# Seven products for all four runs of W_in in the last two groups, and six in-place sums of the second matrix by adding DMAs

## The chip, the cores and the metric

The kernel runs on one core of a Trainium2 chip, in one launch. The metric is the device time of that launch in microseconds (us). Five engines work side by side, each through its own instructions in their order: TensorE (PE in the profile, its weight loads PEld), VectorE (DVE), ScalarE (ACT), GpSimd (POOL) and SyncE (SP). POOL and SP are used here almost only to issue DMAs.

## The reference, cut to what matters

```python
# q, k, v: (4, 8, 768, 64); w_in: (512, 2048); w_out: (2048, 512)
scores = q @ k.T / 8 + bias          # bias by head and distance
scores = where(is_global | is_local, scores, -1e9)   # 8 global keys, 96 local ones
x = softmax(scores) @ v              # heads side by side: (3072, 512)
h = x @ w_in
g = h - tanh(h)
out = g @ w_out                      # (3072, 512), float32
```

## The kernel before

The 3072 rows are 24 tiles of 128 (`u` = 0 to 23). A tile's scores are made against its own 128 keys (block 0) and, where it has one, the tile before it (block 1). `S` are the score matmuls, `E` the exponentials on ACT, `M` the multiplication with a mask on DVE, `AV` the product with v, `R` a reciprocal of the row sums on DVE, `N` the normalisation that writes a tile of x, `Xe` its transposition into `xT` (by PE and a copy up to tile 7, by a DMA from SP after that).

The first matrix product, x @ W_in, takes the tiles in ten groups: two of one tile, five of two tiles and, for tiles 12 to 23, groups 7, 8 and 9 of four tiles (512 rows). The 2048 columns of W_in are 16 slices of 128 (`f`); four slices are a run (`j` = 0 to 3). The direct way for a group of four is `m1`: per slice four matmuls 128x512 into one of the 8 PSUM banks, then tanh on ACT (`th`) and the subtraction h - tanh(h) on DVE (`g`), which writes the bf16 tensor `gall`. The other way takes a run at once as a product of 2 by 2 blocks by seven products instead of eight (`in_product`, `d1` to `d7`, four matmuls 128x256 each). It needs four sums of blocks of W_in per run (`v1` to `v4`, DVE), four of blocks of xT per group (`y1` to `y4`, DVE), three copies out of PSUM per group and run on ACT (`e0` to `e2`) and three additions on DVE (`q11`, `q21`, `q22`: `d_add`). A run so done holds three banks, one of which (`r`) goes to and fro between PE and ACT: product, copy, product, copy, product, copy, product. `DUNITS` lists the pairs (group, run) done in this way: runs 2 and 3 of groups 8 and 9.

The second product, g @ W_out, takes every pair of tiles (a, a + 1) as 2 by 2 blocks, again with seven products (`product`, `p1` to `p7`, eight matmuls 128x256 each), three copies (`a0` to `a2`, `keep`) and four results (`c11` to `c22`), then the stores (`st`) of two tiles of `ot`. Its operands are the blocks of `gall` and four sums of them by DVE (`n1` to `n4`, `g_sum`, 128x1024 bf16): with a11, a12 the first tile's two halves and a21, a22 the second's, n1 = a21 + a22 and n2 = n1 - a11 go to buffers `ss`, n3 = a11 - a21 is written over a21 and n4 = a12 - n2 over a12. `p7` reads n3's result, `p3` that of n4. Sums of blocks of W_out are made once (`w1` to `w4`, `w_sum`).

No scheduler sets the order. The string `ORDER` lists every step by its name, and each engine runs its own steps in the order of that list; a letter behind a slash gives the engine where there is a choice (`a` ACT, `d` DVE, `p` POOL, `s` SP). A second table, `HOMES`, gives each step's buffers and banks.

Of the kernel before, what the change touches and what calls it, by code (L numbers as in the profile page):

```python
# [27 lines left out]
Xe.5/d th.0.12 g.2.14 m1.3.6 E.6.1 g.0.12 m1.3.8 n3.0 th.3.6 lk.10 E.6.0 n2.0 m1.3.4 g.3.6 K.6/a m1.3.2 n1.2 w1.0
m1.3.12 th.3.2 lk.8 g.0.8 th.3.8 p1.0 w1.1 m1.3.10 w3.0 a0.0/a th.3.12 g.3.2 m1.3.0 lv.6 th.3.10 w2.0 p2.0 w2.1 lq.10
w3.1 p6.0 T.7 lv.7 w4.1 p7.0 g.3.8 a1.0/a V.5/a n2.2 p5.0 th.3.0 T.9 n3.2 g.3.12 p1.2 a2.0/a w4.0 p2.2 a0.2/a g.3.10  # L30
th.3.4 p6.2 c11.0 T.8 c22.0 M.6.0 p4.0 a1.2/a n4.2 p5.2 g.3.0 g.3.4 p7.2 a2.2/a c21.0 c11.2 p3.2 st.1.0/p T.10 v1.3
M.6.1 lk.12 S.7 c12.2/a c22.2 lk.14 AV.6 n4.0 E.7.1 p4.2 V.6/d lk.11 R.6 E.7.0 N.6/d m1.3.14 lk.13 M.7.1 X.6 M.7.0
th.3.14 p3.0 lq.12 Xe.6/a c21.2 g.3.14 AV.7 lq.11 c12.0/a K.7/d R.7 S.8 N.7/d lv.8 n1.4 X.7 lv.9 E.8.1 p1.4 Xe.7/d n2.4
lv.10 m1.4.8 E.8.0 v1.2 v2.3 lq.13 m1.4.10 a0.4/a M.8.1 th.4.8 K.9/a p6.4 g.4.8 th.4.10 E.9.0 g.4.10 m1.4.14 a1.4/d S.9
V.7/d th.4.14 M.9.0 T.11 g.4.14 p5.4 E.9.1 M.8.0 T.12 m1.4.4 E.10.0 n3.4 p2.4 M.9.1 st.3.0/s th.4.4 M.10.0 E.10.1 AV.8
n4.4 m1.4.0 T.13 lq.15 K.10/a R.8 a2.4/a N.8/d AV.9 th.4.0 g.4.4 p3.4 Xe.8 R.9 N.9/d m1.4.2 c12.4/a c11.4 Xe.9 m1.4.6
g.4.0 st.4.0/p th.4.2 M.10.1 lq.14 m1.4.12 th.4.6 g.4.2 lv.11 p7.4 g.4.6 th.4.12 lk.15 S.10 c22.4 V.9/d lv.13 g.4.12
p4.4 E.11.0 n1.6 st.2.0/p p2.6 E.12.0 K.11/d lv.12 n3.6 AV.10 n2.6 K.12/a E.11.1 lk.16 p1.6 R.10 c21.4 lq.16 N.10/a
m1.5.10 a0.6/d M.11.1 p6.6 c11.6 th.5.10 S.11 T.15 a1.6/d g.5.10 p5.6 E.13.1 M.12.0 T.14 m1.5.8 V.10/d n4.6 E.13.0
M.11.0 m1.5.14 Xe.10 E.12.1 M.13.1 AV.11 th.5.14 p7.6 R.11 th.5.8 a2.6/d M.12.1 N.11/a m1.5.12 V.11/d v3.2 p3.6 g.5.14  # L40
th.5.12 M.13.0 Xe.11 m1.5.0 c12.6/a c22.6 st.6.0/p g.5.8 m1.5.2 th.5.0 lv.14 T.16 g.5.12 AV.12 g.5.0 th.5.2 lq.19 m1.5.6
R.12 N.12/d lk.18 m1.5.4 th.5.6 g.5.2 lq.18 p4.6 g.5.6 th.5.4 lq.17 g.5.4 S.12 V.12/d lv.16 c21.6 p1.8 n1.8 E.14.1 lv.15
m1.6.4 a0.8/d E.14.0 K.15/d v2.2 lk.17 AV.13 n2.8 th.6.4 m1.6.14 K.14/d lk.19 R.13 E.15.0 g.6.4 p6.8 N.13/d th.6.14 T.18
p2.8 g.6.14 a1.8/a M.14.0 Xe.12 S.13 n4.8 p5.8 c11.8 E.16.1 st.5.0/s v4.3 M.14.1 m1.6.10 E.16.0 M.15.0 T.17 AV.14 n3.8
E.15.1 m1.6.12 R.14 N.14/d T.19 th.6.10 m1.6.0 M.15.1 m1.6.2 a2.8/d th.6.0 Xe.14 M.16.0 V.14/a m1.6.6 g.6.0 th.6.2 Xe.13
g.6.10 AV.15 th.6.6 m1.6.8 g.6.2 g.6.6 p3.8 th.6.8 R.15 N.15/d th.6.12 p7.8 c12.8/a g.6.8 Xe.15 K.16/a st.8.0/p p1.10
g.6.12 lv.19 c22.8 S.14 n1.10 a0.10/a lq.21 n2.10 p4.8 E.17.1 lv.17 M.16.1 p6.10 E.17.0 V.15/d lk.20 p2.10 a1.10/d lk.23
v4.2 c21.8 p5.10 K.17/d lk.21 n4.10 st.9.0/s AV.16 M.17.1 a2.10/a lv.18 E.18.0 m1.7.15 R.16 N.16/d lq.22 p3.10 th.7.15
c11.10 lq.20 g.7.15 S.15 V.16/d c12.10/d lk.22 m1.7.6 M.17.0 E.19.0 lq.23 m1.7.7 E.19.1 M.19.0 lv.20 m1.7.5 M.18.0
# [73 lines left out]
def kernel(  # L123
# [517 lines left out]
    def keep(e, a, k):  # L641
        copy(e, buf(("sn", a, k)), bank(("r", a))[:, 0:DH2])
# [187 lines left out]
```

## Time and profile before

| | |
|---|---|
| median of 3 runs | 202.43 us (202.15 to 202.67) |
| the profiled execution, time and span | 202.65 us and 200.9 us |
| granted TensorE clock | 1.0 |
| busy: PE, DVE, ACT, POOL | 194.4, 178.5, 132.6, 72.9 us |
| bytes moved by DMA | 27.36 MB |

The span is what the trace shows of the kernel from its first to its last event; 1.75 us of the profiled execution's time lie around it. Busy time is the time in which at least one of an engine's instructions ran. Since an instruction's successor on DVE or PE can begin before it ends, the distance from start to start, where an engine works without a gap, says better than the duration how much time an instruction takes up.

### The profile page before, as it was taken

The page shows a single profiled execution, that of the slowest core. Times are in us where ns is not written, and L with a number is a line of the kernel's source. Part 1 is how long each engine was busy: PE and PEld are TensorE (multiplying, and loading weights), DVE is VectorE, ACT ScalarE, POOL GpSimd, SP SyncE. Part 2 cuts the span into 40 slices and gives each one's busy share as a digit, 9 for nine tenths or more (in the row PEclk, how much of TensorE's full clock was granted, in tenths as well). Part 3 has the DMA queues.
Part 4 walks back from the last instruction along what each step waited for, and adds up shares of the span by engine and source line. Part 5 has one row for each costly group of instructions (what it writes and reads, how often), then busy time and mean ns, then how long its engine had stood idle before and what let it go on. Part 6 is the DMA issues. An engine that isn't in the chain of part 4 may idle for free.

```text
span 200.9 us, 5510 instructions
## 1 busy us (share of the span) xinstructions
PE 194.4 (97%) x2195; PEld 155.5 (77%) x2195; DVE 178.5 (89%) x375; ACT 132.6 (66%) x245; POOL 72.9 (36%) x93
## 2 busy tenths in 40 slices
PE   8998999999999999999999999999999999999993
PEld 2567888888878988988898655687877688778882
DVE  6685598999999998999999999999999999999841
ACT  3796889844578678958674785589678774823220
POOL 8995575350693195097009910005100002000011
PEclk9999999999999999999999999999999999999999
DMA  5999999999999999999999999932924112002223
GB/s 145 217 184 184 195 166 207 198 156 145 144 194 161 192 160 182 131 169 152 207 155 145 167 156 167 210 28 58 74 51 110 66 43 104 0 3 106 90 96 131
DMA packets 103755, 27.36 MB, mean 136 GB/s; under 512 B 93921, under 2 KB 101345, under 8 KB 103729
## 3 DMA queue, kind: packets, MB, share of 16 engines
q0 software_dynamic: 73680, 15.54, 85.9%
q1 hardware_dynamic: 29504, 10.95, 30.8%
q10 hardware_dynamic: 544, 0.52, 1.0%
q8 instruction: 17, 0.28, 0.5%
q14 instruction: 10, 0.07, 0.1%
HBM read 27.26 MB, written 6.29 MB: 167 GB/s over the span
## 4 chain that ended last, share of the span: by engine, by line
PE 69%; DMA 13%; DVE 8%; POOL 7%; issue 1%; ACT 0%; POOLq 0%; DVEq 0%
PE ps L636 31%; PE ps L470 24%; DMA w_out_bf<-in_moe_w_out_dram 7%; DMA w_in_bf<-in_moe_w_in_dram 6%; PE ps L529 6%; PE ps L420 4%; PE ps L394 4%; DVE gall L581 2%; POOL w_in_bf L343 2%; POOL vb L340 2%; POOL mem L337 1%; DVE mem L405 1%; DVE wc L608 1%; DVE ot L650 1%; DVE gall L621 1%
## 5 line engine op out<-in xcount | busy, mean ns | idle before, releaser
L470 PE MATMUL ps<-xT,w_in_bf 128*128 128x256 bf16 (+2 forms) x576 | 77.2, 284 | 1.0 <-DMA w_in_bf<-in_moe_w_in_dram 0.9
L470 PEld LDWEIGHTS <-w_in_bf 128*128 128x128 bf16 x576 | 50.2, 98 | 15.9 <-DMA w_in_bf<-in_moe_w_in_dram 1.1
L567 ACT ACTIVATE th<-ps 128x512 f32<-128x512 f32 (+1 forms) x82 | 47.1, 594 | 16.8 <-PE ps L470 14.6
L581 DVE TENSOR_TENSOR gall<-ps,th 128x512 bf16<-128x512 f32 (+1 forms) x82 | 52.9, 667 | 5.9 <-ACT th L567 5.2
L636 PEld LDWEIGHTS <-gall 128*128 128x128 bf16 x488 | 46.3, 98 | 7.6 <-issue 0.5
L401 ACT ACTIVATE mem<-ps 128x1024 bf16<-128x1024 f32 x44 | 43.3, 1027 | 7.9 <-PE ps L394 7.0
L653 POOL DMA_DIRECT2D out_dram<-ot x10 | 5.7, 572 | 105.2 <-DVE ot L650 66.9
L636 PE MATMUL ps<-w_out_bf,gall 128*128 128x256 bf16 (+1 forms) x296 | 36.4, 270 | 0.4 <-ACT ot L272 0.4
L405 DVE TENSOR_TENSOR mem<-mem,mk 128x1024 bf16<-128x1024 bf16 x40 | 26.3, 680 | 0.0
L636 PE MATMUL ps<-f,ss 128*128 128x256 bf16 x192 | 24.9, 273 | 0.0
L636 PE MATMUL ps<-wc,gall 128*128 128x256 bf16 x192 | 24.9, 273 | 0.0
L272 ACT COPY sn<-ps 128x256 f32<-128x256 f32 x23 | 8.6, 372 | 20.8 <-PE ps L636 20.8
L340 POOL DMA_DIRECT2D vb<-in_v_dram x24 | 21.5, 907 | 1.8 <-ACT sn L272 1.6
L340 POOL DMA_DIRECT2D mem<-in_q_dram x20 | 18.0, 908 | 9.5 <-PE ps L420 5.4
L636 PEld LDWEIGHTS <-ss 128*128 128x128 bf16 x192 | 18.4, 98 | 3.2
L340 POOL DMA_DIRECT2D mem<-in_k_dram x20 | 18.1, 915 | 4.6 <-DMA w_out_bf<-in_moe_w_out_dram 3.7
L650 DVE TENSOR_TENSOR ot<-ps,sn 128x256 f32<-128x256 f32 x36 | 14.6, 416 | 4.1 <-PE ps L636 3.1
L420 PEld LDWEIGHTS <-mem 128*128 128x128 bf16 x352 | 13.4, 97 | 2.3 <-ACT mem L401 0.5
L437 DVE TENSOR_TENSOR x<-ps,rden 128x512 bf16<-128x512 f32 x21 | 14.4, 687 | 0.6
L420 PE MATMUL ps<-vb,mem 128*128 128x65 bf16 x352 | 14.7, 193 | 0.1
L394 PE MATMUL ps<-mem 64*128 64x128 bf16 x352 | 13.2, 217 | 0.3 <-DVE gall L581 0.3
L394 PEld LDWEIGHTS <-mem 64*128 64x128 bf16 x352 | 10.0, 94 | 3.4 <-issue 2.4
(76 smaller groups left out, 195.6 us busy)
## 6 DMA issues: line engine op xcount, KB each, us to landing
out_dram<-ot SPq DMA_DIRECT2D x14, 256.0 KB, 2.5
vb<-in_v_dram POOLq DMA_DIRECT2D x24, 128.0 KB, 5.4
mem<-in_q_dram POOLq DMA_DIRECT2D x22, 128.0 KB, 5.8
mem<-in_k_dram POOLq DMA_DIRECT2D x22, 128.0 KB, 5.5
out_dram<-ot POOLq DMA_DIRECT2D x9, 256.0 KB, 2.6
w_out_bf<-in_moe_w_out_dram POOLq DMA_DIRECT2D x4, 512.0 KB, 10.7
w_in_bf<-in_moe_w_in_dram POOLq DMA_DIRECT2D x4, 256.0 KB, 8.2
w_in_bf<-in_moe_w_in_dram POOLq DMA_DIRECT2D x2, 512.0 KB, 11.5
```

Source lines behind the costliest of these rows:

```text
L340: eng(e).dma_start(out=dst, in_=rows_of(src, u).rearrange("h p d -> p h d"))
L394: nc.tensor.matmul(bank(("s", u, o), hh)[:, p * P : (p + 1) * P], buf(("qk", back[u] if o else u))[r, 1, p, :], buf(("qk", u))[r, 0, p, :] ...
L401: nc.scalar.activation(d, banks(("s", u, o), 0, 1), AF.Exp, bias=0.0, scale=scale)
L405: nc.vector.tensor_tensor(out=t, in0=t, in1=mk[:, mask_of(u, o)], op=ALU.mult)
L420: nc.tensor.matmul(t[:, h // (H // 2), h % (H // 2), :], buf(("p", u, o))[:, slot(h), :], buf(("v", back[u] if o else u))[:, h, 0 : Dh + 1 ...
L437: nc.vector.tensor_tensor(out=buf(("x", u)).rearrange("q (a h) d -> q a h d", a=2), in0=t[:, :, :, 0:Dh], in1=rden.to_broadcast([P, 2, H / ...
L470: nc.tensor.matmul(t[:, (f - f0) * n : (f - f0 + 1) * n], w_in_bf[j][:, c, fo : fo + P], x[:, c, 0:n], start=(c == 0), stop=(c == CD - 1),)
L529: nc.tensor.matmul(t[:, r * 2 * P : (r + 1) * 2 * P], w(r)[:, c], x[:, c], start=first and r + c == 0, stop=c == 1, skip_group_check=not f ...
L567: nc.scalar.activation(h_view(buf(("th", g, f0)), g, m), h_view(bank(("h", g, f0)), g, m), AF.Tanh, bias=0.0, scale=1.0)
L581: nc.vector.tensor_tensor(out=o, in0=v(h), in1=v(th), op=ALU.subtract)
L636: nc.tensor.matmul(bank((holder, a))[:, c0:c1], s(f), t(f)[:, c0:c1], start=first and f == 0, stop=f == HF - 1, skip_group_check=not first,)
L650: nc.vector.tensor_tensor(out=o, in0=bank((holder, a))[:, 0:DH2], in1=buf(("sn", a, k)), op=ALU.add)
```

## The change

- `DUNITS` takes all four runs of groups 8 and 9, eight units instead of four. No direct block (`m1`) of these groups is left. `v1` to `v4` are made for runs 0 and 1 too.
- The first tile of each pair (even `u`) is carried negated. Up to tile 7 the copy behind the transposition negates it (`minus`); from tile 8 on, the normalisation does (`a_N`, two SCALAR_TENSOR_TENSOR of half a tile instead of one TENSOR_TENSOR). h - tanh(h) is odd, so the first tile's blocks in `gall` are negated as well, and n2, n3 and n4 become plain additions. The signs are put right in the sums of W_out (`w2` becomes a SCALAR_TENSOR_TENSOR), in `keep` and in `result`.
- n3 and n4 of the pairs 14, 16 and 18, six sums, are DMAs from POOL that add their source to their destination in SBUF (`accum_op`); the other n3 and n4 stay on DVE.
- `ORDER` and `HOMES` are written anew, with other sides for some copies: of the 13 copies `sn` on DVE 4 are left there (one of them negating), of its 11 copies of `vb` 5; the rest goes to ACT.

```diff
 ORDER = """
...
-c12.20/a st.20.0/s p3.22.0 c21.22 c12.22.0/a p3.22.1 st.23.0/s st.22.256/p c12.22.1/d st.22.384/s
...
+p3.22.0 c12.20/a p4.22 st.20.0/s c12.22.0/a st.22.256/s p3.22.1 c21.22 c12.22.1/d st.23.0/s st.22.384/s
...
-    DUNITS = [(8, 2), (8, 3), (9, 2), (9, 3)]
+    DUNITS = [(8, 0), (8, 1), (8, 2), (8, 3), (9, 0), (9, 1), (9, 2), (9, 3)]
...
+    def minus(e, out, in_):
+        if e is ACT:
+            nc.scalar.activation(out, in_, AF.Copy, bias=0.0, scale=-1.0)
+        else:
+            eng(e).tensor_scalar(out=out, in0=in_, scalar1=-1.0, scalar2=None, op0=ALU.mult)
...
+        if u % 2 == 0 and u >= PE_X:
+            for a in range(2):
+                nc.vector.scalar_tensor_tensor(
+                    out=buf(("x", u))[:, a * H // 2 : (a + 1) * H // 2, :], in0=t[:, a, :, 0:Dh], scalar=-1.0,
+                    in1=rden[:, a].to_broadcast([P, H // 2, Dh]), op0=ALU.mult, op1=ALU.mult,
+                )
+            return
...
-        a, b = {1: (b12, b11), 2: (b22, w_half(1, x)), 3: (b22, b12), 4: (b21, w_half(2, x))}[k]
-        nc.vector.tensor_tensor(out=w_half(k, x), in0=a, in1=b, op=ALU.subtract)
+        if k == 2:
+            nc.vector.scalar_tensor_tensor(
+                out=w_half(2, x), in0=w_half(1, x), scalar=-1.0, in1=b22, op0=ALU.mult, op1=ALU.subtract)
+            return
+        a, b, o = {1: (b11, b12, ALU.subtract), 3: (b12, b22, ALU.subtract), 4: (b21, w_half(2, x), ALU.add)}[k]
+        nc.vector.tensor_tensor(out=w_half(k, x), in0=a, in1=b, op=o)
...
-            2: (lambda: buf(("ss", a, 2)), lambda: buf(("ss", a, 1)), lambda: a11, ALU.subtract),
-            3: (lambda: a21, lambda: a11, lambda: a21, ALU.subtract),
-            4: (lambda: a12, lambda: a12, lambda: buf(("ss", a, 2)), ALU.subtract),
+            2: (lambda: buf(("ss", a, 2)), lambda: buf(("ss", a, 1)), lambda: a11),
+            3: (lambda: a21, lambda: a21, lambda: a11),
+            4: (lambda: a12, lambda: a12, lambda: buf(("ss", a, 2))),
...
-        nc.vector.tensor_tensor(out=o(), in0=x(), in1=y(), op=op)
+        if e is POOL:
+            nc.gpsimd.dma_start(out=o(), in_=y(), accum_op=ALU.add)
+            return
+        nc.vector.tensor_tensor(out=o(), in0=x(), in1=y(), op=ALU.add)
...
-        nc.vector.tensor_tensor(out=o, in0=bank((holder, a))[:, 0:DH2], in1=buf(("sn", a, k)), op=ALU.add)
+        x, y = bank((holder, a))[:, 0:DH2], buf(("sn", a, k))
+        nc.vector.tensor_tensor(out=o, in0=y if k == 0 else x, in1=x if k == 0 else y, op=ALU.subtract)
...
-            op((f"n{k}", a), DVE, lambda e, a=a, k=k: g_sum(a, k))
+            op((f"n{k}", a), DVE if k < 3 else None, lambda e, a=a, k=k: g_sum(e, a, k))
```

Where the sums of pair 16 are made, in the middle of group 9's tiles, DVE's row of instructions before the change reads as follows (`ss1_107<-ss2_108,gall` is n2, `gall<-gall` n3; L543 and L540 are `d_add`, L650 and L274 a result and a copy of a pair before).

```order
L621 TENSOR_TENSOR ss1_107<-ss2_108,gall_105 128x1024
L543 TENSOR_TENSOR mem_81<-ps_61,mem_81 128x512
L540 TENSOR_TENSOR ps_61<-ps_61,mem_81 128x512
L650 TENSOR_TENSOR ot2_118<-ps_61,sn3_114 128x256
L274 COPY sn0_111<-ps_61 128x256
L543 TENSOR_TENSOR mem_81<-ps_61,mem_81 128x512
L621 TENSOR_TENSOR gall_105<-gall_105 128x8x128
```

The same place on DVE in the changed kernel, with n1 and n2 of pair 16 (L647), `d_add` (L558) and the sums of xT (L525):

```order
L677 TENSOR_TENSOR ot2_118<-ps_61,sn1_112 128x256
L647 TENSOR_TENSOR ss2_108<-gall_105 128x1024
L525 TENSOR_TENSOR mem_81<-xT1_98,mem_81 128x512
L558 TENSOR_TENSOR ps_61<-ps_61,mem_81 128x512
L525 TENSOR_TENSOR mem_81<-xT1_98 128x512
L647 TENSOR_TENSOR ss1_107<-ss2_108,gall_105 128x1024
L677 TENSOR_TENSOR ot1_117<-sn0_111,ps_61 128x256
```

n3 and n4 of this pair are gone from DVE, its copy too, and the additions of the units stand in their place.

POOL's row near its end before the change, three loads of v and then stores:

```order
L340 DMA vb1_83<-in_v_dram 128x8x64
L340 DMA vb6_88<-in_v_dram 128x8x64
L340 DMA vb2_84<-in_v_dram 128x8x64
L653 DMA out_0_dram<-ot2_118 128x512
L653 DMA out_0_dram<-ot3_119 128x512
```

POOL's row near its end now, from n4 of pair 16 on; the rows of L645 are the adding DMAs:

```order
L645 DMA gall_105<-ss1_107 128x8x128
L680 DMA out_0_dram<-ot3_119 128x512
L645 DMA gall_105<-gall_105 128x8x128
L645 DMA gall_105<-ss2_108 128x8x128
L680 DMA out_0_dram<-ot1_117 128x512
L680 DMA out_0_dram<-ot2_118 128x512
```

Behind the last load POOL now has the six adding DMAs and three stores, and nothing else.

SP's last rows before the change; the last one is the store of the last 128 columns of tile 22, the one ahead of it the whole tile 23:

```order
L653 DMA out_0_dram<-ot0_116 128x256
L653 DMA out_0_dram<-ot1_117 128x512
L653 DMA out_0_dram<-ot3_119 128x512
L653 DMA out_0_dram<-ot0_116 128x128
L825 UNCONDITIONAL_BRANCH
```

SP's last rows now:

```order
L680 DMA out_0_dram<-ot3_119 128x512
L680 DMA out_0_dram<-ot2_118 128x512
L680 DMA out_0_dram<-ot1_117 128x128
L680 DMA out_0_dram<-ot0_116 128x512
L680 DMA out_0_dram<-ot1_117 128x128
```

The store of the third quarter of tile 22 has come over from POOL; tile 23 (`ot0_116`) and the last quarter end the row as before.

More of the change, by code (lines that the diff above doesn't have):

```diff
@@ L28 @@
[L28 to L37, printed above, removed]
@@ L455, in a_Xe @@
     def a_Xe(e, u):
-        copy(e, x_dst(u), bank(("xt", u)).bitcast(BF16)[:, 0 : CD * P].rearrange("q (c f) -> q c f", c=CD))
+        (minus if u % 2 == 0 else copy)(
+            e, x_dst(u), bank(("xt", u)).bitcast(BF16)[:, 0 : CD * P].rearrange("q (c f) -> q c f", c=CD))
     def a_DX(u):
@@ L641, in keep @@
     def keep(e, a, k):
-        copy(e, buf(("sn", a, k)), bank(("r", a))[:, 0:DH2])
+        (minus if k == 0 else copy)(e, buf(("sn", a, k)), bank(("r", a))[:, 0:DH2])
     def result(e, a, i, j, c0=0, c1=DH2):
```

182 lines of the change are left out of this document (98 added, 84 removed).

## The prediction

> **What bounds the kernel now.** I read the page's first part, the chain of waits, the table of windows, and then single rows of the timeline, the groups and the DMAs.
>
> ```profile
> span 200.9 us, 5510 instructions
> PE 194.4 (97%) x2195; PEld 155.5 (77%) x2195; DVE 178.5 (89%) x375; ACT 132.6 (66%) x245; POOL 72.9 (36%) x93
> PE 69%; DMA 13%; DVE 8%; POOL 7%; issue 1%; ACT 0%; POOLq 0%; DVEq 0%
> 179.73 17.05 PE ps L636 x160
> ```
>
> PE is busy for all but 6.5 us of the span, and the chain that ended last runs through it: 69% of the chain is PE, at its end 17.05 us of pair products (L636) without a break. DVE has 22.4 us free on the whole, but the windows say where. Their columns are the stretch, then the busy time of PE, PEld, DVE, ACT and POOL with the instructions in brackets, then clock, DMA share and GB/s.
>
> ```profile
> 0.00:24.00 24.00, 21.59 (x267) 15.10 (x267) 14.81 (x53) 16.90 (x27) 19.24 (x28) 1.00 1.41 187
> 24.00:41.00 17.00, 16.81 (x243) 14.99 (x237) 16.07 (x30) 14.47 (x26) 8.46 (x11) 1.00 1.70 187
> 41.00:66.00 25.00, 24.61 (x293) 21.33 (x291) 24.66 (x49) 15.69 (x28) 11.97 (x14) 1.00 2.08 158
> 66.00:136.00 70.00, 69.99 (x845) 55.50 (x843) 66.82 (x139) 49.99 (x92) 27.80 (x33) 1.00 1.48 158
> 136.00:181.00 45.00, 45.00 (x408) 34.12 (x407) 44.22 (x85) 31.31 (x66) 4.35 (x6) 1.00 0.30 57
> 181.00:197.70 16.70, 16.34 (x157) 14.51 (x154) 11.67 (x24) 4.26 (x12) 0.87 (x2) 1.00 0.28 104
> ```
>
> From 66 us to the last matmul PE never stands still except for 0.4 us near the end. DVE is the second bound: 66.8 of 70 us, then 44.2 of 45 us in the stretch of groups 8 and 9, and it is free only in the last 17 us (11.7 of 16.7). So a cut on PE counts in full unless it loads DVE, and where it loads DVE between 136 and 181 there are 0.8 us to take it up.
>
> **The change part by part.** *The products.* How much time a matmul takes up is read from start to start in an unbroken row of PE; the columns are start, length, engine, line, operation and count.
>
> ```profile
> 98.60 3.65 PE L470 MATMUL ps<-xT,w_in_bf 128*128 128x256 bf16 x32
> 102.09 0.65 PE L420 MATMUL ps<-vb,mem 128*128 128x65 bf16 x16
> 121.43 3.62 PE L470 MATMUL ps<-xT,w_in_bf 128*128 128x512 bf16 x16
> 124.89 1.04 PE L636 MATMUL ps<-wc,gall 128*128 128x256 bf16 x8
> ```
>
> 32 matmuls of 256 columns take 102.09 - 98.60 = 3.49 us, 0.109 each; 16 of 512 columns take 124.89 - 121.43 = 3.46 us. The latter are just a direct unit (16 slices by group: four slices of four matmuls). By sevenths it is 28 x 0.109 = 3.05 us. Four units: 4 x 0.41 = **1.6 us less on PE**, all of it on the chain.
>
> *DVE's bill.* Pace first: rows of 512 columns out of PSUM follow each other at 0.60 us, two of 256 in 0.66.
>
> ```profile
> 155.07 0.68 DVE L581 TENSOR_TENSOR gall<-ps,th 128x512 bf16<-128x512 f32 x1
> 155.67 0.68 DVE L543 TENSOR_TENSOR mem<-ps,mem 128x512 f32<-128x512 f32 x1
> 156.27 0.68 DVE L581 TENSOR_TENSOR gall<-ps,th 128x512 bf16<-128x512 f32 x1
> 51.04 0.75 DVE L650 TENSOR_TENSOR ot<-ps,sn 128x256 f32<-128x256 f32 x2
> 51.70 0.42 DVE L502 TENSOR_TENSOR mem<-w_in_bf 128x512 bf16<-128x512 bf16 x1
> ```
>
> The groups' rows give, behind the count, busy time and mean length; an operation as long as one of these (0.68 or 0.41) is taken at the same pace (0.60 or 0.33).
>
> ```profile
> L540 DVE TENSOR_TENSOR ps<-ps,mem 128x512 f32<-128x512 f32 x4 | 2.7, 684 | 0.0
> L543 DVE TENSOR_TENSOR mem<-ps,mem 128x512 f32<-128x512 f32 x8 | 5.5, 685 | 0.3 <-ACT mem L272 0.2
> L502 DVE TENSOR_TENSOR mem<-w_in_bf 128x512 bf16<-128x512 bf16 x4 | 1.6, 411 | 0.0
> L621 DVE TENSOR_TENSOR gall<-gall 128x1024 bf16<-128x1024 bf16 x12 | 8.2, 684 | 0.0
> L274 DVE COPY sn<-ps 128x256 f32<-128x256 f32 x13 | 5.4, 414 | 1.3 <-PE ps L636 1.3
> L274 DVE COPY vb<-vb 8x512 bf16<-8x512 bf16 x11 | 4.3, 394 | 0.0
> L284 DVE SCALAR_TENSOR_TENSOR far<-rel,far 128x256 bf16<-128x256 bf16 x1 | 0.4, 426 | 0.0
> L285 DVE TENSOR_TENSOR dist<-far,rel 128x256 bf16<-128x256 bf16 x1 | 0.3, 291 | 0.0
> L272 ACT COPY mem<-ps 128x512 f32<-128x512 f32 x12 | 6.9, 589 | 2.9 <-PE ps L529 2.8
> ```
>
> Added are 12 `d_add` (12 x 0.60 = 7.2) and 8 sums of W_in (2.6). Gone are six n3 and n4 (3.6), nine copies `sn` (3.0) and six of `vb` (about 0.3 each, 1.8). The two sums `w2` become SCALAR_TENSOR_TENSOR. The one such row took 426 ns for 256 bf16 elements where TENSOR_TENSOR took 291, as long as a 256-column f32 operation, so I take it at one element a step: 1.13 us for 1024 instead of 0.60, together +1.1 (bounds 0, as TENSOR_TENSOR, and 2.2). The eight normalisations in halves cost 0.66 instead of 0.60, and one more goes to ACT: even (0 to 1). Sum: 7.2 + 2.6 - 3.6 - 3.0 - 1.8 + 1.1 = **+2.5 us on DVE**. A tensor operand from PSUM or f32 is at one rate and bf16 from SBUF at twice that in these rows (684 ns for 512 and for 1024).
>
> *Where it falls.* By the new order the eight sums of W_in and the lighter copies lie ahead of 136 us, where DVE has 3.2 us free of 70; the two long sums lie between 41 and 66 us, where the new order has about 1.7 us less of other work on DVE (two g, a mask, a sum n and two copies of `vb` fewer, some smaller steps more), which covers their 1.1. I take both at nothing (bounds -0.4 and +0.5: 0.39 us of PE's time is idle there, and DVE has 0.34 free). Between product 7 of pair 12 and product 7 of pair 18, the stretch 136 to 181, PE now has 56 sevenths and 21 pair products instead of 28, 16 direct slices and 19: 56 x 0.436 + 21 x 0.873 = 42.7 against 12.2 + 13.8 + 16.6 = 42.6, so it stays as long, and the 1.6 us come off the last stretch, which has two pair products fewer. On DVE it gains 12 `d_add` and a mask (+7.8), and loses seven sums n, three copies and a normalisation (-4.2 - 1.0 - 0.6): +2.0. 44.2 + 2.0 is 46.2 us of work in 45.1: 1.1 us too much. A part can be pushed on into the last 17 us, since what PE has made can wait in other banks; I take half of it, **+0.6** (bounds 0, and 1.1 + 0.8 = 1.9 if DVE keeps all of its present waits).
>
> *The adding DMAs.* No such DMA is in the trace. The nearest rows:
>
> ```profile
> mem<-in_q_dram POOLq DMA_DIRECT2D x22, 128.0 KB, 5.8
> out_dram<-ot POOLq DMA_DIRECT2D x9, 256.0 KB, 2.6
> w_out_bf<-in_moe_w_out_dram POOLq DMA_DIRECT2D x4, 512.0 KB, 10.7
> ```
>
> In pieces it is like the loads of q (1024 of them; 5.8 us to landing, with the DMAs full). From issue to its reader the order leaves on PE: n3 of pair 16 13 sevenths and 2 products, 13 x 0.436 + 2 x 0.873 = 7.4 us; n4 of pair 18 4 and 7, 7.9; n4 of 14 9.7; the others 10.9 and more. At 5.8 us all are hidden: 0. Bounds: 2.6 us, and 10.7, by which n3 of pair 16 alone would hold up `p7` by 3.3. Only stores stand behind them on POOL. ACT gains 12 copies of 0.589, nine of `sn` and six of `vb`, some 14 us in all, on 132.6 of 200: hidden.
>
> *The end.* Columns as in the timeline, then two DMA rows.
>
> ```profile
> 195.29 1.04 PE L636 MATMUL ps<-wc,gall 128*128 128x256 bf16 x8
> 196.37 0.42 DVE L650 TENSOR_TENSOR ot<-ps,sn 128x256 f32<-128x256 f32 x1 [1.27 <-PE ps L636]
> 196.81 0.27 ACT L272 COPY ot<-ps 128x128 f32<-128x128 f32 x1 [0.95 <-PE ps L636]
> 197.13 0.61 PE L636 MATMUL ps<-w_out_bf,gall 128*128 128x128 bf16 x8 [0.35 <-ACT ot L272]
> 197.84 0.29 DVE L274 COPY ot<-ps 128x128 f32<-128x128 f32 x1 [1.05 <-PE ps L636]
> out_dram<-ot SPq DMA_DIRECT2D x14, 256.0 KB, 2.5
> out_dram<-ot SPq DMA_DIRECT2D x1, 64.0 KB, 1.6
> ```
>
> Before, the last half product waited 0.35 us for ACT's copy out of its bank. Now `p4` of pair 22 (0.87 us) stands between the halves: **-0.35**. But tile 23's store waits for `c21`, which follows `p4`. Its result, done 0.95 us ahead of PE's end before (196.79 to 197.74), now comes about at PE's end, and 256 KB take 2.5 us, while the last quarter leaves 0.45 after the end and takes 1.6. The last landing moves from 2.05 to about 2.55 us behind PE: **+0.5**.
>
> Sum: -1.6 + 0.6 + 0 - 0.35 + 0.5 = -0.85, from the profiled 202.65 (span 200.9 and 1.75 around it) to 201.8. That run lay 0.22 above the median of 202.43, so the median to expect is **201.6 us**.
>
> **The rivals.** *DVE and the banks take over (slower).* Place: 136 to 181 us. For it: 98% there now, and a direct slice asks one bank once, while each added unit asks ACT for three copies (12 more of 0.589), each between two products in one bank; with no direct slices left, only other units and pair products can fill in. Against: in the list of waits PE stands behind none of the 12 copies of before, and ACT has 13.7 of the 45 us free. Price: the full 1.9 instead of 0.6, and a quarter of each added copy uncovered, 12 x 0.15 = 1.8, together 3.1 more: 204.7; at half of the copies' part 203.8. It decides from 2.0 us of loss in that stretch on. I take 203.8.
>
> *The adding DMAs land late.* For it: in-place addition has to read its destination too. At 9.5 us, n3 of pair 16 would be 2.1 late and n4 of pair 18 1.6, less what the first wait gives the second: 2 to 3 us, 203.8 to 204.6; at 8.5 us 202.9. Against: the DMAs are at 0.30 of their share in that stretch (the windows' column), where the 5.8 us were measured at 1.4 to 2. The Trainium skill, SBUF — State Buffer, Who interferes with whom, says that a DVE copy in a two-port mode locks GpSimd out while it writes a DMA's descriptors, and infers that a TENSOR_TENSOR does not. By that rule only the odd copy of `vb` could delay an adding DMA here, and the result would be the forecast. No run here shows it yet. The Trainium skill, DMA: Bandwidth & Descriptors, Anatomy of one DMA, fits a DMA of GpSimd by 2.0 us plus its bytes at 436 GB/s; for 256 KB that is an estimate of 2.6 us, which the stores' row matches and the loads' row does not, and the sum would be the same.
>
> *All of the gain.* DVE's waits fill up and the work of 41 to 66 us runs freer: 201.6 - 0.6 - 0.4 = 200.6. Against: a reciprocal and its normalisation, one behind the other, can't overlap.
>
> *The sevenths bring nothing*, since 28 weight loads replace 16: 202.4. Against: a load stays under a matmul's 0.109 us in the 32-row above, which already has one load for each matmul.
>
> **How the numbers follow.** Forecast 0.40 (201.0 to 202.2; 0.33 of it below 201.8), DVE and banks 0.30 (0.25 slower, 0.05 the same), all of the gain 0.13, late DMAs 0.09 (0.07 slower), nothing 0.08 (the same, 0.01 slower). About 0.3%, 0.6 us, can be told from no change: below 201.8 is faster, above 203.0 slower. Faster 0.46, same 0.21, slower 0.33. The range goes from 200.4, a little under all of the gain, to 203.9, the slower rival's own value. The forecast's own range is 201.0 to 202.2.
>
> **What would show it.** Right: PE without gaps from 66 us to its end, in a stretch from product 7 of pair 12 to that of pair 18 about as long as now; DVE near 45 us busy there; adding DMAs landing in 3 to 7 us; PE's last wait for ACT gone; SCALAR_TENSOR_TENSOR of 1024 near 1.2 us. Wrong: waits of PE or PEld for ACT or DVE in that stretch adding up to over 2 us, PE waiting for `gall` from a DMA, or a last store that lands more than 3 us behind PE.

## The result and the profile after

The changed kernel takes 203.39 us (median of 22 runs, 202.81 to 205.06) where the kernel before takes 202.21 us (22 runs beside it): 1.0063 of it, 95% interval 1.0045 to 1.0080. In a second set it was 1.0043 (1.0021 to 1.0065). So it is slower by 0.9 to 1.2 us where 0.8 us faster was forecast; the time lies inside the prediction's outer range (200.4 to 203.9) but outside the forecast's own (201.0 to 202.2), and the direction was wrong. The profiled execution took 203.98 us, with a span of 202.2.

The first rows of the page of the changed kernel, the span, the engines and the chain of waits:

```profile
span 202.2 us, 5685 instructions
PE 194.1 (96%) x2243; PEld 159.3 (79%) x2243; DVE 179.9 (89%) x381; ACT 145.2 (72%) x280; POOL 82.3 (41%) x99
PE 65%; DMA 15%; DVE 7%; POOL 7%; ACT 3%; issue 2%; SPq 1%; POOLq 0%; DVEq 0%
```

DVE has 1.4 us more to do, ACT 12.6, and POOL 9.4 (its adding DMAs); PE's share of the chain is smaller, ACT's is no longer nothing. For the question where the time is, fixed stretches of the clock serve badly, since the work in them moves. I cut the run at two products that both orders have: product 7 of pair 12 and product 7 of pair 18. Their first rows in the timeline, before and after:

```profile
135.15 0.27 PE L636 MATMUL ps<-wc,gall 128*128 128x256 bf16 x1
180.44 0.27 PE L636 MATMUL ps<-wc,gall 128*128 128x256 bf16 x1
```

```profile
136.03 0.27 PE L662 MATMUL ps<-wc,gall 128*128 128x256 bf16 x1
183.30 0.27 PE L662 MATMUL ps<-wc,gall 128*128 128x256 bf16 x1
198.18 0.61 PE L662 MATMUL ps<-w_out_bf,gall 128*128 128x128 bf16 x8
```

The table of windows for just these stretches (stretch, then busy PE, PEld, DVE, ACT, POOL), before:

```profile
135.15:180.44 45.29, 45.29 (x410) 34.40 (x408) 44.51 (x85) 31.80 (x65) 4.35 (x6) 1.00 0.33 58
180.44:197.74 17.30, 16.94 (x162) 15.00 (x159) 12.23 (x25) 4.61 (x12) 0.91 (x2) 1.00 0.27 102
```

And after:

```profile
136.03:183.30 47.27, 46.55 (x475) 40.49 (x473) 46.19 (x89) 39.65 (x88) 11.56 (x9) 1.00 0.74 85
183.30:198.79 15.49, 15.26 (x146) 13.25 (x143) 11.68 (x24) 4.32 (x12) 1.18 (x2) 1.00 0.29 106
```

The middle stretch is 1.98 us longer, the last one 1.81 shorter. Behind PE's last matmul the span runs on for 202.2 - 198.79 = 3.41 us, 3.16 before. Behind 136 us the change thus costs 0.4 us, and what is left of the 0.9 to 1.2 lies ahead of it. The middle stretch is not longer because PE has more to do there: its 392 matmuls of 256 columns take 42.7 us at 0.109 each, and before 264 of them and 64 of 512 columns (0.216 each) took 42.6. The 80 small matmuls for scores and AV, 2.3 us from start to start, are the same. So PE's work is 45.0 of 47.27 us, where it was 44.9 of 45.29, and about 1.9 of the 1.98 us are waits. In five profiled runs with this order behind 136 us (this one, e1, e2, e4 and e9 below) the middle stretch is 47.25 to 47.29 us; the start of product 7 of pair 12, in contrast, lay at 136.03 in this run and at 134.47 in another of the very same kernel (e9).

### The profile page after: what moved, and what is told of

Same layout as the page of the kernel before. It is cut to its first block, busy times and chain, and to the rows that moved or that the text cites. A ratio compares the mean times of both kernels' runs of the same rounds, so it can differ in the third digit from the quotient of the medians.

```text
span 202.2 us, 5685 instructions
## 1 busy us (share of the span) xinstructions
PE 194.1 (96%) x2243; PEld 159.3 (79%) x2243; DVE 179.9 (89%) x381; ACT 145.2 (72%) x280; POOL 82.3 (41%) x99
## 4 chain that ended last, share of the span: by engine, by line
PE 65%; DMA 15%; DVE 7%; POOL 7%; ACT 3%; issue 2%; SPq 1%; POOLq 0%; DVEq 0%
PE ps L662 29%; PE ps L488 18%; PE ps L547 10%; DMA w_in_bf<-in_moe_w_in_dram 6%; DMA w_out_bf<-in_moe_w_out_dram 6%; PE ps L404 4%; PE ps L430 4%; DVE gall L578 3%; DMA xT<-x 3%; ACT th L572 2%; POOL w_in_bf L353 2%; POOL vb L350 2%; POOL mem L347 1%; DVE mem L561 1%; POOL mem L350 1%
## 5 line engine op out<-in xcount | busy, mean ns | idle before, releaser
L488 PE MATMUL ps<-xT,w_in_bf 128*128 128x256 bf16 (+2 forms) x512 | 61.2, 273 | 1.1 <-DMA xT<-x 1.1
L488 PEld LDWEIGHTS <-w_in_bf 128*128 128x128 bf16 x512 | 43.7, 98 | 11.8 <-issue 1.3
L585 ACT ACTIVATE th<-ps 128x512 f32<-128x512 f32 (+1 forms) x66 | 37.1, 585 | 16.3 <-PE ps L488 15.3
L599 DVE TENSOR_TENSOR gall<-ps,th 128x512 bf16<-128x512 f32 (+1 forms) x66 | 42.1, 665 | 4.7 <-ACT th L585 4.2
L680 POOL DMA_DIRECT2D out_dram<-ot x10 | 6.6, 659 | 62.8 <-DVE ot L677 36.8
L276 ACT COPY mem<-ps 128x512 f32<-128x512 f32 (+1 forms) x29 | 16.6, 592 | 4.0 <-PE ps L547 3.5
L276 ACT COPY sn<-ps 128x256 f32<-128x256 f32 x21 | 7.8, 372 | 12.1 <-PE ps L662 12.1
L430 PEld LDWEIGHTS <-mem 128*128 128x128 bf16 x352 | 13.7, 97 | 2.3 <-ACT mem L411 0.5
L547 PEld LDWEIGHTS <-mem 128*128 128x128 bf16 x128 | 12.3, 97 | 2.4 <-issue 0.5
L547 PE MATMUL ps<-mem 128*128 128x256 bf16 x96 | 13.2, 272 | 0.4 <-DVE gall L578 0.4
```

The lines of the kernel that those rows point to most:

```text
L276: nc.scalar.copy(out=out, in_=in_)
L430: nc.tensor.matmul(t[:, h // (H // 2), h % (H // 2), :], buf(("p", u, o))[:, slot(h), :], buf(("v", back[u] if o else u))[:, h, 0 : Dh + 1 ...
L488: nc.tensor.matmul(t[:, (f - f0) * n : (f - f0 + 1) * n], w_in_bf[j][:, c, fo : fo + P], x[:, c, 0:n], start=(c == 0), stop=(c == CD - 1),)
L547: nc.tensor.matmul(t[:, r * 2 * P : (r + 1) * 2 * P], w(r)[:, c], x[:, c], start=first and r + c == 0, stop=c == 1, skip_group_check=not f ...
L585: nc.scalar.activation(h_view(buf(("th", g, f0)), g, m), h_view(bank(("h", g, f0)), g, m), AF.Tanh, bias=0.0, scale=1.0)
L599: nc.vector.tensor_tensor(out=o, in0=v(h), in1=v(th), op=ALU.subtract)
```

## The experiments

Two theories stood against each other for the middle stretch. **A:** DVE has more work there than the stretch has time. **B:** PE asks for a bank before the chain over ACT and DVE has given it back, wherever the order has put it, and the load matters little. PE's waits there are small, in these five runs at the same places, and the larger ones are hand-overs. The timeline of the changed kernel at the clearest of them:

```profile
167.05 0.60 PE L547 MATMUL ps<-xT,mem 128*128 128x256 bf16 x4
167.69 0.60 ACT L572 ACTIVATE th<-ps 128x512 f32<-128x512 f32 x1 [0.62 <-PE ps L547]
168.18 0.69 DVE L558 TENSOR_TENSOR ps<-ps,mem 128x512 f32<-128x512 f32 x1
168.18 0.58 ACT L276 COPY mem<-ps 128x512 f32<-128x512 f32 x1
168.65 0.61 ACT L572 ACTIVATE th<-ps 128x512 f32<-128x512 f32 x1
169.30 1.29 DVE L578 TENSOR_TENSOR gall<-ps,th 128x512 bf16<-128x512 f32 x2 [0.43 <-ACT th L572]
169.67 0.60 PE L547 MATMUL ps<-xT,mem 128*128 128x256 bf16 x4
170.64 0.60 PE L547 MATMUL ps<-mem 128*128 128x256 bf16 x4 [0.37 <-DVE gall L578]
```

A seventh ends at 167.65; tanh, a copy of another unit, a second tanh, then two g on DVE, and at 170.64 the bank goes to `d7` of the next unit. From the product's end to the bank are 3.0 us. Four matmuls take up 0.436 us, so `d7` could have come at 169.67 + 0.44 = 170.11 and came 0.53 late (the row's 0.37 counts from the modelled end). The first g had its tanh at 168.29 and DVE was free from 168.87 on, but it started at 169.30, with the end of the second tanh; why is not shown. In the same way AV of tile 22 comes 0.41 us late, `p1` of pair 16 with `p4` of pair 14 behind it 0.43, and `p6` of pair 20, in the last stretch, 0.39. All late starts between 136 and 190 us add up to 2.4 us, leaving out those under 0.06.

**The sums back on DVE (e3).**

```diff
-n3.14/p   -n4.14/p   -n3.16/p   -n4.16/p   -n3.18/p   -n4.18/p
+n3.14/d   +n4.14/d   +n3.16/d   +n4.16/d   +n3.18/d   +n4.18/d
```

> The changed kernel with the six adding DMAs made on DVE at the same places of the order (6 x 0.60 = 3.6 us more on DVE between 137 and 178 us). Theory A (DVE's throughput bounds the stretch of groups 8 and 9): 2.5 to 3.6 us slower than the change. Theory B (what PE waits for there is the latency of the chain product, copy or tanh on ACT, addition or subtraction on DVE, bank free, and DVE has slack between): 0 to 1.5 us slower.

Measured: 205.77 us, 1.0157 (1.0114 to 1.0199), span 204.4. The middle stretch is 49.95 us, 2.7 more than with the change, for 3.6 us of work, and DVE is busy in nearly all of it (the same columns):

```profile
135.50:185.45 49.95, 47.36 (x474) 40.54 (x472) 49.39 (x95) 40.07 (x88) 2.23 (x3) 1.00 0.29 49
```

So the adding DMAs carry a load that DVE has no room for, as A says. In the time it is a good 2 us slower than the changed kernel (3.2 over the kernel before, against 0.9 to 1.2): a little under A's 2.5, well over B's 1.5.

**Order at the four places (e8).** On top of e1 (below), with the steps between left out here; beside it ran the changed kernel itself (e9).

```diff
-AV.22 ... V.22/a ... d4.8.0      -g.8.2 ... c22.14     -d7.9.1 th.9.1 d3.9.1      -p6.20 ... p2.22
+d4.8.0 AV.22 V.22/a              +c22.14 ... g.8.2     +d3.9.1 th.9.1 d7.9.1      +p2.22 ... p6.20
```

> The changed kernel with Xe.12 ahead of Xe.13 and five words moved where PE waits: AV.22 behind d4.8.0, c22.14 ahead of g.8.2, d3.9.1 ahead of d7.9.1, p2.22 ahead of p6.20; the same work. Theory B (each of the four waits is the latency of one hand-over of a PSUM bank, with PE work at hand that the order puts too late): the four waits shrink from 1.8 us to under 0.6, the run is 1.5 to 2.4 us shorter than the change, 0.3 to 1.2 us shorter than the kernel before. Theory A (DVE's throughput is the bound there): the waits come back at the next places, the four together with their successors stay above 1.3 us, and only the 0.5 to 1 us of Xe.12 come out.

> The changed kernel itself, as a measure for the other runs of this chip. Ratio to before 1.004 to 1.008. Its waits of PE at AV.22, p4.14, d7.9.1 and p6.20 (0.41, 0.45, 0.53, 0.39 us in the first trace) should be there again to within 0.05 us; the wait for xT at the first product of group 7 (1.21 us there) should vary.

Measured: 203.77 us, 1.0069 (1.0048 to 1.0090), no faster than e9's 203.08, 1.0043 (1.0021 to 1.0065). The waits named were gone or smaller except that of `p1.16` and `p4.14` (now 0.50, all of it at `p1.16`), and new ones stood at `d4.8.0` (0.52) and `d1.9.3` (0.22): the middle stretch went from 47.26 in e9 to 47.62. Moving the waiting steps did not buy the time back here.

**Xe of tile 12 (e1), w2 without the long operation (e2), both (e4).** These are about the part ahead of 136 us. In the changed order SP has the transposition of tile 12 behind three others and two of its own kind. The timeline of SP and PE:

```profile
98.50 6.23 SPq L385 DMA_TRANSPOSE mem<-mem  x3
104.83 3.84 SPq L477 DMA_TRANSPOSE xT<-x  x3
112.87 0.81 PE L488 MATMUL ps<-xT,w_in_bf 128*128 128x512 bf16 x3 [1.05 <-DMA xT<-x]
```

Its x was ready at 89.3 us, and PE's first product of group 7 waited for it at 112.87. e1 and e2 (e4 has both):

```diff
# e1
-Xe.13 ... Xe.14 ... Xe.15 ... Xe.12
+Xe.12 Xe.13 ... Xe.14 ... Xe.15
# e2: w2 by a plain operation, with w3 ahead of it in the order
-nc.vector.scalar_tensor_tensor(out=w_half(2, x), in0=w_half(1, x), scalar=-1.0, in1=b22, ...)
+nc.vector.tensor_tensor(out=w_half(2, x), in0=w_half(3, x), in1=b11, op=ALU.subtract)
```

> The changed kernel with one word of the order moved: the transposition Xe.12 stands ahead of Xe.13 on SP instead of behind Xe.15. Theory (SP's queue): tile 12's x is ready at 89.3 us and its transposition waits in the queue until 107.4; ahead of Xe.13 it starts near 95, the last of the four is then Xe.15 at about 106, PE's wait of 1.1 us at 112 us goes and the run is 1.0 us (0.8 to 1.3) shorter than the change, ratio to before about 1.001. Rival (the DMAs are full there and any last transposition lands late): the wait stays above 0.6 us, gain under 0.5 us.

> The changed kernel with the sum w2 made as w3 - b11 by TENSOR_TENSOR, w3 standing ahead of it; same results. Theory (the SCALAR_TENSOR_TENSOR of 1024 elements runs one element at a time, and DVE sets the pace between 40 and 46 us): two instructions get 0.53 to 0.64 us shorter, the 1.15 us that PE loses at 41 to 43 us fall to under 0.6, the run is 0.4 to 0.6 us shorter than the change. Rival (PE waits there for the landing of W_out): the loss stays, gain under 0.2 us.

> Both edits, Xe.12 ahead of Xe.13 and w2 by TENSOR_TENSOR. If the two waits are independent the gains add up: 1.4 to 1.7 us shorter than the change, 0.2 to 0.5 us shorter than the kernel before (ratio 0.998). If an earlier group 8 only waits longer for ACT and DVE in the stretch behind, less than 1.0 us comes out.

Measured: 203.25 us, 1.0030 (1.0000 to 1.0060); 203.37, 1.0037 (1.0011 to 1.0063); 203.24, 1.0038 (1.0011 to 1.0066), beside the kernel before at 202.54. The gains expected (1.0, 0.4 to 0.6, and 1.4 to 1.7 us) did not come: none of the three can be told from e9. In their traces the late start at group 7 (1.22 us with the change) is down to 0.2 in e1 and e4, and that at `p6` of pair 0 (0.43) is gone in e2. But this does not show that the edits did it. In e9, the same kernel without an edit, group 7 is late by 0.2 only: its last transposition landed 2.9 us behind its issue there and 5.2 in the trace above. And `p6` of pair 0 is late by 0.49 in e4, which has e2's edit, and not at all in e1, which hasn't. The waits of this part come and go from run to run; both are shown in one trace, and neither their cause in the order nor their worth in the time is shown.

**Less work on each engine (e5, e6, e12, e10, e15).** All with e1's order, each profiled once; what is cut is left out.

```diff
# e5: additions q21, q22 of the units
-        nc.vector.tensor_tensor(out=a, in0=d_bank(g, j, "z"), in1=a, op=ALU.add)
+        nc.vector.tensor_tensor(out=a[:, 0:DH2], in0=d_bank(g, j, "z")[:, 0:DH2], in1=a[:, 0:DH2], op=ALU.add)
# e6: tanh of the units
-        nc.scalar.activation(o, h_of(g, f), AF.Tanh, bias=0.0, scale=1.0)
+        nc.scalar.activation(o[:, 0:1], h_of(g, f)[:, 0:1], AF.Tanh, bias=0.0, scale=1.0)
# e12: copies e0, e1, e2
-        copy(e, d_keep(g, j, k), d_bank(g, j, "r"))
+        copy(e, d_keep(g, j, k)[:, 0:DH2], d_bank(g, j, "r")[:, 0:DH2])
# e10: e5 and e6.   e15: all three and q11
```

> The changed kernel with Xe.12 ahead of Xe.13, and the additions q21 and q22 done on 256 of their 512 columns only (the other half of h is left without its sum). 16 x 0.27 = 4.3 us less on DVE between 142 and 180 us. Theory A (DVE's throughput): the waits at AV.22, p4.14 and d7.9.1 go, 1.2 to 1.5 us shorter than with Xe.12 moved alone. Theory B (latency of the hand-over, of which these additions are only a part): less than 0.7 us shorter, d7.9.1 (tanh and copies on ACT ahead of it) keeps over 0.3 us.

> The changed kernel with Xe.12 ahead of Xe.13, and the tanh of the eight units done on 256 of their 512 columns only (the subtraction takes old values for the rest). 32 x 0.21 = 6.8 us less on ACT between 148 and 186 us. If ACT's part of the hand-over counts (theory B): the wait at d7.9.1 falls from 0.53 to under 0.2 us and that at p6.20 from 0.39 to under 0.2, 0.6 to 1.2 us shorter than with Xe.12 moved alone. Theory A (DVE's throughput): less than 0.4 us shorter.

> With the order of e1; the 24 copies on ACT that the units make out of their banks (e0, e1, e2) on 256 of 512 columns, the rest of them left out; tanh and additions whole. About 6 us less on ACT, and the chain product, copy, addition is 0.2 us shorter at each copy. Halved tanh cut the waits of PE between 136 and 190 us from 2.4 to 1.2 us. If that was ACT's load, the copies do as much: 1.4 us or less of waits. If it was the length of tanh itself, between a product and the g that frees its bank, the copies do little: 1.9 us or more.

> With the order of e1, and both cuts at once: the additions q21 and q22 of the units on 256 of 512 columns, and the tanh of the units on 256 of 512 columns (the rest of these is left out). Waits of PE between 136 and 190 us were 2.4 us with the first cut alone and 1.2 with the second alone. If they come of the load on DVE and ACT together, they fall to 0.2 to 0.6 us, and PE ends 0.6 to 1.0 us earlier than with the second cut alone. If they come of fixed chains from a product over ACT and DVE to the bank that is asked for next, which a free engine does not shorten, 1.0 us or more stays.

> With the order of e1; every step of the units on ACT and DVE but g cut to 256 of 512 columns: the three copies, the three additions and tanh (the rest of them left out). The stretch from product 7 of pair 12 to that of pair 18 took 45.30 us before, 47.29 with e1, 46.26 with tanh halved, 45.99 with tanh and two of three additions halved, 46.89 with the copies halved; its work on PE alone is as long as before. If the units' steps on ACT and DVE make all of the 2 us, it comes to 45.3 to 45.6. If something else in the new order makes part of them, it stays at 45.8 or more.

Measured, each kernel's row of windows from product 7 of pair 12 to that of pair 18, in the order e5, e6, e12, e10, e15:

```profile
135.10:182.22 47.12, 46.40 (x474) 40.46 (x472) 42.78 (x90) 39.23 (x88) 11.55 (x9) 1.00 0.75 85
```

```profile
135.75:182.01 46.26, 45.99 (x475) 40.47 (x472) 45.86 (x89) 34.24 (x88) 11.54 (x9) 1.00 0.76 87
```

```profile
135.48:182.37 46.89, 46.40 (x474) 40.50 (x472) 46.15 (x89) 35.02 (x88) 11.55 (x9) 1.00 0.75 86
```

```profile
134.69:180.69 46.00, 45.90 (x475) 40.48 (x473) 42.66 (x90) 33.91 (x88) 11.55 (x9) 1.00 0.77 87
```

```profile
135.12:180.91 45.79, 45.79 (x475) 40.43 (x473) 40.62 (x90) 29.24 (x88) 11.55 (x9) 1.00 0.77 88
```

DVE at 42.78 instead of 46.19 us shortens the stretch by 0.15 only, and AV of tile 22 and `d7` are as late as before (0.41 and 0.53): against A as the sole cause. The same 4.6 to 5.4 us off ACT is worth 1.0 as a shorter tanh and 0.4 as shorter copies: not ACT's load, but the length of the step between a product and the bank. (With tanh short `d7` is 0.27 late, where under 0.2 was expected.) With tanh short, DVE's 45.86 fill all but 0.40 of the stretch, and lighter additions are now worth 0.26. The late starts of e10, some 0.9 us counted as above, lie between its two theories. With all three kinds cut the stretch is 45.79, between the two bounds expected, and 0.50 over before: 1.5 of the 1.98 us hang on these steps. Of the 0.50, 0.1 is PE's own work, as counted above, and 0.4 are waits of at most 0.13 us each, whose cause stays open. So there are two limits, one close under the other: the hand-over over tanh alone holds the stretch at 47.1 (e5), DVE's work alone at 46.3 (e6). These are single traces; five of one order agreed within 0.04 us.

**Normalisations of tiles 21 and 23 on DVE (e13).** With e1's order.

```diff
-N.21/a   -N.23/a
+N.21/d   +N.23/d
```

> With the order of e1, and the normalisations of tiles 21 and 23 on DVE (one operation of about 0.7 us each) instead of ACT (eight small ones, 1.75 us in a row each). ACT has 3.5 us less, DVE 1.2 us more, in the stretch from 143 to 157 us. If ACT's queue makes PE wait there, the waits of AV.22 and p4.14 (0.41 and 0.44 us) shrink, those between 136 and 190 us are 1.9 us or less and the time is 202.3 to 202.9, a gain over e1. If DVE is at its end there, they grow by up to 1.2 us and the time is 203.3 to 204.4.

Measured: 204.6 us, 1.0109 (1.0075 to 1.0142), 0.2 above the slower of the two forecasts. Nearly 3 us off ACT gain nothing, and 1.2 us more on DVE cost 1.16:

```profile
135.12:183.55 48.43, 46.87 (x475) 40.47 (x472) 47.35 (x91) 36.76 (x72) 11.55 (x9) 1.00 0.73 83
```

**Half of the units undone (e11).** Units 0 and 1 of group 9 as eight direct slices, with e1's order.

```diff
-    DUNITS = [(8, 0), (8, 1), (8, 2), (8, 3), (9, 0), (9, 1), (9, 2), (9, 3)]
+    DUNITS = [(8, 0), (8, 1), (8, 2), (8, 3), (9, 2), (9, 3)]
+h.9.0:2 h.9.4:6 h.9.1:3 h.9.5:7 h.9.2:2 h.9.3:3 h.9.6:6 h.9.7:7
```

One slice's tanh takes the buffer of slice 10 of group 8 a step early, so that slice 10's values are of the wrong tanh; no step is left out.

> With the order of e1, but units 0 and 1 of group 9 as eight direct slices again, in the banks of these units (2, 3, 6, 7) and put where their products stood. PE has 0.8 us more to do, ACT six copies less, DVE six additions less (3.6 us). If the added units cause the waits, those between 136 and 190 us fall from 2.4 to at most 1.2 us, with d7.9.1's gone, and the time is 202.5 to 203.0, no slower than e1 (203.25). If the order around them causes the waits, they stay at 1.9 or more and the time is 203.8 or more.

Measured: 203.9 us, 1.0071 (1.0049 to 1.0093). The middle stretch became 48.04 us, 0.75 longer than e1's 47.29: PE's added 0.8 us came in full and the waits stayed, though DVE (43.18) and ACT (36.84) had some 3 us less in it. `d7.9.2` (0.50 late) waited in place of `d7.9.1`. About 1.5 of the 2.4 us of late starts up to 190 us lie ahead of these units, so that only the rest could answer; it did not fall. By what was expected this speaks for the order around the units and not the units themselves as the cause. But this is one hand-written order, and a better one for two units may exist.

**Signs and adding DMAs alone, in the order before (e7, e14).** e7 has the order, banks and four direct runs of before, the signs, and all six adding DMAs where n3 and n4 stood; tile 20 is normalised on ACT there without its sign. e14 has four adding DMAs, n3 of pair 14 behind POOL's last load of v, and tile 20's sign in place.

```diff
# e14 against e7
-n3.14/p lv.23 ... lv.21 ... lv.22    -n4.16/p   -n4.18/p   -N.20/a
+lv.23 ... lv.21 ... lv.22 n3.14/p    +n4.16/d   +n4.18/d   +N.20/d
```

> The kernel before with its own order, its four direct runs and its banks, and only two things of the change: the signs (with what they need in operations), and the six sums n3 and n4 of pairs 14, 16 and 18 as adding DMAs on POOL. PE does the same work as before; DVE has 3.6 us less of sums and about 1 us more of long SCALAR_TENSOR_TENSOR. If the adding DMAs and the signs are free, the time is that of before within 0.4 us, and PE waits no more than 0.5 us in all between 136 us and its last product (0.7 before, of it 0.5 at the very end). The rival, that the adding DMAs or the signs carry the cost: 0.6 us or more over before, with PE waiting for ss or gall from a DMA.

> As e7: the order, direct runs and banks of the kernel before, the signs of the change and adding DMAs, but only four of these (n3 and n4 of pair 14, n3 of pairs 16 and 18), each with 6 us or more to its reader, and n3 of pair 14 behind the last load of v on POOL; n4 of pairs 16 and 18 on DVE. If signs and adding DMAs are free where they have their room, the time is that of before within 0.5 us (202.0 to 203.0 where before is 202.45), with PE waiting for no DMA behind 136 us. If they cost on their own, it is 203.1 or more.

Measured: e7 211.08 us, 1.0412 (1.0380 to 1.0445), beside 202.45. The timeline of its POOL and PE shows two costs of adding DMAs in bad places:

```profile
140.12 1.62 POOL L641 DMA_DIRECT2D gall<-gall  x1
141.03 3.37 POOL L346 DMA_DIRECT2D vb<-in_v_dram  x3
148.18 0.51 PE L426 MATMUL ps<-vb,mem 128*128 128x65 bf16 x11 [0.86 <-DMA vb<-in_v_dram]
181.40 3.09 POOL L641 DMA_DIRECT2D gall<-ss  x2 [4.02 <-PE ps L658]
189.46 6.46 PE L658 MATMUL ps<-w_out_bf,gall 128*128 128x256 bf16 x32 [4.00 <-DMA gall<-ss]
195.76 1.04 PE L658 MATMUL ps<-f,ss 128*128 128x256 bf16 x8
```

n3 of pair 14 stands ahead of three loads of v in POOL's queue. They were issued 0.9 us later than in e14, where they stand ahead of it, and landed 6.2 us behind their issue instead of 3.4 to 4.2, so that AV of tile 21 came 1.03 us late. (In both runs POOL comes to them only at 140 us, since it waits for a store ahead of them.) n4 of pairs 18 and 16, issued from 181.40 on, let PE wait until 189.46, 8 us later; the second of them was issued at 182.29 and landed 7.1 us after that. After that wait of 4 us, 32 matmuls took 195.76 - 189.46 = 6.30 us, 0.197 each instead of 0.109. e14: 204.28 us, 1.0087 (1.0053 to 1.0122) beside 202.38, outside its first theory. Not through the adding DMAs: its middle stretch is 45.52 us (45.29 before), its last 17.30 (17.30 before). So the cost must lie ahead: product 7 of pair 12 starts at 136.74, 1.6 us later than before (a start that moves from run to run, but the time itself is 1.9 us up), and in the waits from 41 to 66 us stand the long sum w2 and the g behind it, with a wait for xT later. e7 has the same two waits from 41 to 66 us (for f and for gall, 0.4 each), and the kernel before has neither, so they go with the signs in this order; the sum w2 is one of the operations that the signs made longer. What else the signs cost ahead of 136 us is not split. The list of waits of PE in e14, from 41 to 66 and then from 100 to 190 us:

```profile
PE ps L658 <- DVE f L622: 0.4, 1, 0.4
PE ps L658 <- DVE gall L595: 0.4, 1, 0.4
...
PE ps L484 <- DMA xT<-x: 0.7, 1, 0.7
```

No version that does the whole work beats the kernel before.

## Why the prediction was wrong, and where it was right

**DVE in the middle stretch, the step that failed.** The text put 46.2 us of work for DVE against 45.1 us of stretch, and the trace has 46.19 busy. (That these agree so well is in part luck: the text went from 44.2 between 136 and 181 us and added 2.0; between the two products DVE had 44.51 and gained 1.68, and in the whole run it gained 1.4, not 2.5.) Of the two bounds it then gave, 0 and 1.9, it took 0.6, on the argument that a part "can be pushed on into the last 17 us, since what PE has made can wait in other banks". Measured is 1.98, the upper bound and a little more. Nothing was pushed on: 47.27 - 46.19 = 1.08 us of DVE are idle, where 0.78 were before. Other banks were not to be had where it can be followed: the bank that `d7` waits for above is one of two that a unit keeps until tanh and g of two slices have read them. And DVE itself waits for ACT's tanh inside the stretch, for 0.8 of its 1.08 idle us, time that the sum counted as usable. The groups of DVE in the stretch show it:

```profile
L578 DVE TENSOR_TENSOR gall<-ps,th 128x512 bf16<-128x512 f32 x14 | 9.0, 681 | 0.9 <-ACT th L572 0.8
```

The rival of that name had the place right, and its point of decision (2.0 us of loss) was missed by a hair (1.98). The sign that the text gave for being wrong, over 2 us of PE's waits there, is met when they are counted from start to start (47.27 - 45.0); the list of waits, which counts from modelled ends, shows 0.6. Its price was not: the quarter of each added copy, 1.8 us, did not come on top; halving all 24 copies gave 0.4. What made the hand-over long was most of all tanh in the chain (1.0 for half of it), which the rival did not name.

**The products.** 56 sevenths in place of 28 and 16 slices were forecast to leave the middle stretch as long and to take 1.6 us off the last. The last stretch lost 1.81 where 1.6 + 0.35 was forecast. That the middle stretch stays as long for PE's own work holds: 45.0 us against 44.9. The gain on PE was real and all of it was spent on DVE and the hand-over.

**The last wait and the stores.** The wait for ACT between the two halves of pair 22's last product is gone: `p4` of pair 22 (197.31) runs straight into the half (198.18). New is the 0.39 us of `p6` of pair 20, for n2 on DVE. The end behind PE grew by 0.25, not 0.5: tile 23's store landed 2.0 us behind its issue, not 2.5, and the last to land was still the last quarter of tile 22. The timeline of the changed kernel, PE's last products and that wait:

```profile
188.06 0.94 PE L662 MATMUL ps<-f,ss 128*128 128x256 bf16 x7 [0.23 <-DVE ss L647]
...
197.31 1.04 PE L662 MATMUL ps<-wc,gall 128*128 128x256 bf16 x8
198.18 0.61 PE L662 MATMUL ps<-w_out_bf,gall 128*128 128x128 bf16 x8
```

**The adding DMAs.** Forecast at 5.8 us to landing and hidden; they land in 5.5 and 5.1 (medians), and PE waits for none. The Trainium skill, DMA: Bandwidth & Descriptors, Anatomy of one DMA, gave an estimate of 2.6 us; the trace has twice that, so by these rows the bytes alone do not give it. The DMA rows of the changed kernel:

```profile
gall<-gall POOLq DMA_DIRECT2D x3, 256.0 KB, 5.5
gall<-ss POOLq DMA_DIRECT2D x3, 256.0 KB, 5.1
```

The rival "late" did not come about here; e7 shows what it would have cost.

**Ahead of 136 us.** Forecast at nothing, with -0.4 to +0.5. The long operation took the length forecast, and it does show: `p6` of pair 0 waits for it.

```profile
41.60 1.05 PE L662 MATMUL ps<-w_out_bf,gall 128*128 128x256 bf16 x8 [0.55 <-DMA w_out_bf<-in_moe_w_out_dram]
41.63 1.22 DVE L626 SCALAR_TENSOR_TENSOR f<-f,w_out_bf 128x1024 bf16<-128x1024 bf16 x1 [1.00 <-DVE gall L599]
42.91 1.05 PE L662 MATMUL ps<-f,ss 128*128 128x256 bf16 x8 [0.27 <-DVE f L626]
```

In e9's trace `p6` is late by 0.34 with ACT's tanh as the releaser. SP's queue was not looked at, though `Xe` had moved in it; PE lost 1.2 us there in this trace and 0.2 in e9's. By the medians this part costs 0.5 to 0.8 us (0.9 to 1.2 less 0.4), at or over the upper bound given; no run splits it further, and its cause stays open.

The sum as it came out: -1.8 (last stretch) + 2.0 (middle) + 0.25 (end) + 0.5 to 0.8 (ahead, as the remainder) is +0.9 to +1.2.

## What to carry to other kernels

Where an engine off the critical path was at 98% in a stretch, each microsecond added to it there cost three quarters of one or more (3.6 cost 2.7, 1.2 cost 1.16), whatever room it had later; taking work off it may still bring nothing, if a chain of hand-overs stands at the same height. So price the stretch by the longest of several floors: PE's work, DVE's work plus the waits it now has, and the time from a product to the release of its bank. Of every step that an order moves, follow its queue: in e7 the loads behind an adding DMA on POOL landed about 3 us later than ahead of it. And before a wait in one trace is put down to the order, look for it in a second trace of the same kernel: those from 136 us on came back to within 0.01 us, the one at group 7 did not.

## What the hardware showed beyond the forecast

- An adding DMA of 256 KB inside SBUF kept POOL for about 1.55 us in the changed kernel (three in 4.7 us) and landed 5.1 to 6.0 us behind its issue. Of two issued 0.9 us apart in e7 the second landed 8 us behind the issue of the first.
- A wait of PE of 4.0 us, in e7, was followed by 6.3 us of matmuls at little more than half speed; the table of windows there has a granted clock of 0.54. By these paces the wait cost 2.8 us more than its length (32 x 0.088).

```profile
189.00:195.80 6.80, 6.34 (x33) 4.63 (x34) 0.56 (x1) 0.77 (x2) 0.00 (x0) 0.54 0.16 61
```

The Trainium skill, TensorE: Matmul & The Clock Gate, The HAM clock gate, says that the clock falls to half after at least one idle window of about 3.4 us and comes back after at least one busy window of that length, and that these windows run freely, whatever the kernel does. This case agrees: half the clock after 4.0 us of waiting, and a way back of about 6 us, between one such window and two.
